# Retention plus Mish MLP: the first two tiles regrouped into the first chunks of eight batches

## The chip, the cores and the metric

The kernel runs on one core of a Trainium2 chip. The metric is device time in microseconds (us) of one execution. One profiled execution gives the trace; three others, not profiled, give the time.

The engines are named as the profile names them: PE (TensorE, matrix products; its weight loads are PEld), DVE (VectorE), ACT (ScalarE), POOL (GpSimd) and SP (SyncE, which only issues DMAs here). DMAs are issued from SP, ACT and POOL and are carried out by 16 DMA engines.

## The reference

Inputs are q, k and v of shape (8 batches, 8 heads, 576 positions, 64) in float32, and two weights, 512 x 2048 and 2048 x 512.

```python
scores = (q @ k.transpose(0, 1, 3, 2)) / sqrt(64)
gamma  = 1 - 2.0 ** (-5 - arange(8))                  # one decay per head
Dmat   = where(i >= j, gamma[h] ** (i - j), 0)
x      = ((scores * Dmat) @ v)                        # retention, no softmax
x      = x.transpose(0, 2, 1, 3).reshape(4608, 512)   # tokens x (heads * 64)
h      = x @ w_in                                     # 4608 x 2048
out    = (h * tanh(log1p(exp(h)))) @ w_out            # Mish, then 4608 x 512
```

## The kernel before

**Chunks and tiles.** Each batch has four chunks of 128 positions (c = 0 to 3) and a rest of 64; the rests of two neighbouring batches make one chunk (c = 4). That is 36 chunks, in the order b0: 0, 1, 2, 3; b1: 0, 1, 2, 3; the rests of b0 and b1; b2: 0 and so on (lines 50 to 55). Four chunks in this order make a tile of 512 tokens, the moving size of the first GEMM; there are 9 tiles.

**Attention of one chunk** is done in chunked form: the scores inside the chunk with a causal mask, plus the product of q with a state, the sum of k and v outer products of the earlier chunks of the batch. The decay is put into q and v: q is multiplied by gamma^position (and the scale), v by gamma^-position. The steps have letters in `att` (line 300):

- P, `step_p` (line 155): VectorE multiplies q by its decay into bf16 (`qks`, first half).
- V, `step_v` (161): GpSimd multiplies v by its decay into `vs`; for the first four chunks it also casts k.
- T, `step_t` (170): q and k are transposed into `qkT`. For chunks below `NPE = 16` PE does it through PSUM and ACT copies the result (line 180); for the others a DMA transpose on ACT's queue does it (line 182).
- S, `step_s` (185): PE makes the scores of all heads, two heads at a time on the two halves of its rows; VectorE multiplies them by the mask into `sm` (line 197).
- K, `step_k` (202): PE adds the chunk's outer products to the state in PSUM, ACT copies the state twice into `ssb`, with the unwanted half of each head pair set to zero (line 219).
- O, `step_o` (222): PE adds state times q (unless c = 0) and `vs` times `sm`; VectorE copies the result into `xT`, the transposed input of the first GEMM (line 243).

**The two GEMMs.** `g1(t, f)` (line 249) makes one block of 128 of the 2048 hidden columns for tile t, in 4 matmuls of 512 columns; ACT applies Mish while it moves the block into `gT`. `g2(t, i)` (line 258) makes a quarter of the sum for one chunk of 128 tokens, in 4 matmuls; after the fourth quarter the result is copied to `res` and stored by SP (`store`, line 287). G1 below stands for all 16 `g1` of a tile, G2 for all 16 `g2`.

**Loads.** `load(n)` (line 82) fetches q, k and v of a chunk, in rows of 256 bytes (64 float32 of one head and position). The first four chunks are loaded by SP, 12 DMAs in a row; every later one by GpSimd, whose DMA also casts k to bf16. The weights are loaded by GpSimd with a cast, in four parts each (lines 107 to 111). Buffers for 8 chunks of q and v and for 12 of `qks` let loads run `PF = 7` chunks ahead.

**Order.** The schedule is written out by hand (`manual_schedule`): each engine runs its instructions in the order of the program text.

1. Lines 307 to 317: attention of tile 0, chunk by chunk, between it the parts of w_in.
2. Lines 318 to 323: loads of chunks 4 to 6 and parts of w_out are issued, and G1 of tile 0 runs alone.
3. Lines 325 to 346: three of the four output chunks of tile 0 are accumulated side by side (matmuls at line 343), and attention of chunks 4 to 7 is done between them.
4. Lines 348 to 370: the last output chunk of tile 0, G1 of tile 1 and attention of chunks 8 to 11.
5. Lines 381 to 417: for t = 2 to 9, `g1(t, i)` and `g2(t - 1, i)` alternate, and the attention of the next tile, two chunks per half loop, is placed between them. For t = 2 a table of steps (line 387) brings the loop into this rhythm.
6. Line 418: the last output chunk, in two halves.

Of the kernel before, what the change touches and what calls it, by code (L numbers as in the profile page):

```python
# [10 lines left out]
F32 = mybir.dt.float32  # L11
# [6 lines left out]
def kernel(  # L18
# [28 lines left out]
    NPE = 16  # L47


    chunks = []  # L50
    for b2 in range(0, B, 2):
        for b in (b2, b2 + 1):
            for c in range(4):
                chunks.append((b, c))
        chunks.append((b2, 4))
    nT = len(chunks) // NCH
# [3 lines left out]
    io = ctx.enter_context(tc.tile_pool(name="io", bufs=8))  # L60
# [13 lines left out]


# [5 lines left out]

    def load(n):
        if n >= len(chunks):
            return
        b, c = chunks[n]
        qr = io.tile([P, H, D], F32, name="qraw")
        vr = io.tile([P, H, D], F32, name="vraw")
        qks = io.tile([P, 2, H, D], BF16, name="qks", bufs=12)
        live[n] = {"q": qr, "v": vr, "qks": qks}
        if n < NCH:  # L90
            kr = io.tile([P, H, D], F32, name="kraw", bufs=NCH)
            for t, src in ((qr, q), (kr, k), (vr, v)):
                nc.sync.dma_start(  # L93
                    out=t, in_=src[b, :, ds(P * c, P), :].rearrange("h p d -> p h d"))
            live[n]["k"] = kr
            return
        for t, src in ((qr, q), (qks[:, 1], k), (vr, v)):
            if c < 4:
                nc.gpsimd.dma_start(  # L99
                    out=t, in_=src[b, :, ds(P * c, P), :].rearrange("h p d -> p h d"))  # L100
            else:
                for e in range(2):
                    nc.gpsimd.dma_start(
                        out=t[ds(64 * e, 64)],
                        in_=src[b + e, :, ds(512, 64), :].rearrange("h p d -> p h d"))
# [7 lines left out]
    PF = 7  # L113
    for n in range(NCH):
        load(n)


    ident = consts.tile([P, P], BF16)
# [6 lines left out]
                   allow_small_or_imprecise_dtypes=True)  # L125
    ex = consts.tile([P, 5, H], F32)
    for h in range(H):
        nc.vector.tensor_scalar(ex[:, :, h], pos, math.log(1.0 - 2.0 ** (-5.0 - h)), None, op0=OP.mult)
# [8 lines left out]
    mask = consts.tile([P, P], F32)  # L137
    mask2 = consts.tile([P, P], F32)
    nc.gpsimd.memset(mask, 1.0)
    nc.gpsimd.affine_select(out=mask, in_=mask, compare_op=OP.is_ge, fill=0.0,  # L140
                            base=0, pattern=[[1, P]], channel_multiplier=-1)
    nc.gpsimd.tensor_copy(mask2, mask)
    nc.gpsimd.memset(mask2[0:64, 64:P], 0.0)

# [3 lines left out]
    nc.vector.memset(diag[64:P, 1:2], 1.0)  # L148


    st_ps = {}
    st_sb = {}
    xts = {}

    def step_p(n):
        qr = live[n]["q"]
        c = chunks[n][1]
        nc.vector.tensor_tensor(live[n]["qks"][:, 0], qr,  # L158
                                gq[:, c, :].unsqueeze(2).to_broadcast([P, H, D]), op=OP.mult)

    def step_v(n):
        vr = live[n]["v"]
        if n < NCH:
            nc.gpsimd.tensor_copy(live[n]["qks"][:, 1], live[n]["k"])
        c = chunks[n][1]
        vs = tok.tile([P, H, D], BF16, name="vs")
        nc.gpsimd.tensor_tensor(vs, vr, gv[:, c, :].unsqueeze(2).to_broadcast([P, H, D]), op=OP.mult)  # L167
        live[n]["vs"] = vs

    def step_t(n):  # L170
        flat = live[n]["qks"].rearrange("p i h d -> p (i h d)")
        qk = tr.tile([P, 2, NP, P], BF16, name="qkT", bufs=5)
        if n < NPE:
            if n < NCH:
                tp = ps_h.tile([P, 2 * NP, P], BF16, name="hp")
            else:
                tp = ps_sc.tile([P, 4 * NP, P], BF16, name="sc")[:, 0:2 * NP]
# [3 lines left out]
        else:  # L181
            nc.scalar.dma_start_transpose(out=qk.rearrange("p i n t -> p (i n) t"), in_=flat)  # L182
        live[n]["qk"] = qk

    def step_s(n):

# [8 lines left out]
        sm = tr.tile([P, 2, NP, P], BF16, name="sm")  # L195
# [6 lines left out]
    def step_k(n):  # L202

        if n >= len(chunks):
            return
        b, c = chunks[n]
        if c == 4:
            return
        ks, vs = live[n]["qks"][:, 1], live[n]["vs"]
        if c == 0:  # L210
            st_ps[b] = ps_st.tile([P, NP, 64], F32, name="st")
        st = st_ps[b]
# [4 lines left out]
        ssb = tr.tile([P, NP, 2, 64], BF16, name="ssb", bufs=8)  # L217
        for e in range(2):
            nc.scalar.activation(ssb[:, :, e, :], st, AX.Copy, scale=diag[:, e:e + 1])  # L219
        st_sb[b, c] = ssb  # L220

    def step_o(n):

        b, c = chunks[n]
        t, s = divmod(n, NCH)
        qk, vs, sc, sm = (live[n][x] for x in ("qk", "vs", "sc", "sm"))
        del live[n]
        ot = sc[:, 0]
        if c > 0:
            halves = [(0, P, b, c - 1)] if c < 4 else [(0, 64, b, 3), (64, 64, b + 1, 3)]  # L230
            for i0, iw, bb, cc in halves:
                for p in range(NP):
                    for e in range(2):
                        nc.tensor.matmul(ot[ds(64 * e, 64), p, ds(i0, iw)], lhsT=st_sb[bb, cc][:, p, e, :],  # L234
                                         rhs=qk[:, 0, p, ds(i0, iw)],
                                         start=(i0 == 0 and p == 0), stop=False, skip_group_check=True)
# [212 lines left out]
```

## Time and profile before

| What | Value |
|---|---|
| Median of three runs | 325.55 us (325.14 to 325.85) |
| Span of the profiled execution, first to last instruction | 323.8 us |
| PE busy | 302.4 us, 93% |
| GpSimd busy | 139.2 us, 43% |
| ACT busy | 131.3 us, 41% |
| VectorE busy | 113.0 us, 35% |
| DMA | 43.36 MB, mean 134 GB/s |
| HBM read, written | 36.70 MB, 9.44 MB |
| Start of G1 of tile 0 | 22.34 us |
| Start of the loop for t = 2 | 84.73 us |

The profiled execution has no other time of its own than the span; the three runs lie 1.3 to 2.0 us above it, for what lies before the first and after the last instruction. A busy PE is not a PE at its peak, as matmuls overlap: the spacing of neighbouring matmuls tells their price, 0.216 us for 512 columns where nothing is in the way. The bytes that the profile counts for a DMA with a cast are those written.

The parts of the profile used below: the slices (busy tenths of an engine in 40 equal parts of the span), windows (busy time by engine, then granted clock, DMA share and GB/s), the timeline (instructions with start and length), and the chain of waits (what released the work that ended last, step by step back to the start).

### The profile page before, as it was taken

The page shows a single profiled execution, that of the slowest core. Times are in us where ns is not written, and L with a number is a line of the kernel's source. Part 1 is how long each engine was busy: PE and PEld are TensorE (multiplying, and loading weights), DVE is VectorE, ACT ScalarE, POOL GpSimd, SP SyncE. Part 2 cuts the span into 40 slices and gives each one's busy share as a digit, 9 for nine tenths or more (in the row PEclk, how much of TensorE's full clock was granted, in tenths as well). Part 3 has the DMA queues.
Part 4 walks back from the last instruction along what each step waited for, and adds up shares of the span by engine and source line. Part 5 has one row for each costly group of instructions (what it writes and reads, how often), then busy time and mean ns, then how long its engine had stood idle before and what let it go on. Part 6 is the DMA issues. An engine that isn't in the chain of part 4 may idle for free.

```text
span 323.8 us, 5627 instructions
## 1 busy us (share of the span) xinstructions
PE 302.4 (93%) x2345; PEld 150.3 (46%) x2384; DVE 113.0 (35%) x154; ACT 131.3 (41%) x232; POOL 139.2 (43%) x168
## 2 busy tenths in 40 slices
PE   1779999989999899999999999999999999999995
PEld 1544445444545445444544454445444444444444
DVE  2640055354544425152425343443434232000111
ACT  5435734367746324334434432334243432333200
POOL 4596858999998717372717184202010000000000
PEclk9999999999999999999999999999999999999999
DMA  9999999999999979979999999404040401000031
GB/s 171 215 165 215 227 213 196 254 226 181 172 217 212 189 145 119 174 131 191 111 173 106 203 90 197 105 32 99 32 99 32 100 32 34 32 32 34 33 97 65
DMA packets 81833, 43.36 MB, mean 134 GB/s; under 512 B 68880, under 2 KB 73232, under 8 KB 81808
## 3 DMA queue, kind: packets, MB, share of 16 engines
q0 software_dynamic: 42816, 25.17, 51.8%
q1 hardware_dynamic: 17728, 12.46, 14.5%
q10 hardware_dynamic: 21264, 5.38, 12.3%
q8 instruction: 18, 0.29, 0.4%
q14 instruction: 7, 0.06, 0.1%
HBM read 36.70 MB, written 9.44 MB: 142 GB/s over the span
## 4 chain that ended last, share of the span: by engine, by line
PE 85%; DVE 6%; issue 2%; SPq 2%; DMA 2%; ACT 2%; ACTq 1%; POOL 0%; DVEq 0%
PE hp L254 37%; PE ops L269 31%; DVE sm L197 3%; PE sc L193 3%; PE sc L239 2%; PE sc L234 2%; PE hp L269 2%; SPq L93 2%; PE sc L179 2%; PE st L215 2%; DVE qks L158 2%; DMA kraw<-in_k_dram 2%; PE hp L343 1%; PE hp L281 1%; ACTq L182 1%
## 5 line engine op out<-in xcount | busy, mean ns | idle before, releaser
L254 PE MATMUL hp<-xT,w_in_t 128*128 128x512 bf16 x544 | 143.7, 384 | 3.9 <-DVE xT L243 1.0
L256 ACT ACTIVATE gT<-hp 128x512 bf16<-128x512 f32 x144 | 84.9, 597 | 134.3 <-PE hp L254 100.8
L269 PE MATMUL ops<-w_out_t,gT 128*128 128x512 bf16 x477 | 122.2, 379 | 1.2 <-ACT res L289 0.7
L254 PEld LDWEIGHTS <-w_in_t 128*128 128x128 bf16 x576 | 54.1, 99 | 65.3 <-issue 5.2
L269 PEld LDWEIGHTS <-gT 128*128 128x128 bf16 x512 | 50.0, 98 | 61.6 <-issue 2.0
L289 DVE COPY res<-ops 128x512 f32<-128x512 f32 x30 | 20.7, 691 | 144.8 <-PE ops L269 140.7
L167 POOL TENSOR_TENSOR vs<-vraw,gv 128x512 bf16<-128x512 f32 x36 | 38.7, 1080 | 40.4 <-PE sc L239 24.0
L197 DVE TENSOR_TENSOR sm<-sc,mask 128x1024 bf16<-128x1024 f32 x36 | 42.8, 1217 | 18.7 <-PE sc L193 18.7
L99 POOL DMA_DIRECT2D qraw<-in_q_dram x28 | 26.2, 934 | 36.4 <-DVE qks L158 35.6
L219 ACT ACTIVATE ssb<-st,diag 128x256 bf16<-128x256 f32 x64 | 26.8, 470 | 23.4 <-PE st L215 23.4
L243 DVE CAST xT<-sc 128x512 bf16<-128x512 f32 x36 | 23.7, 686 | 22.0 <-PE sc L239 21.9
L158 DVE TENSOR_TENSOR qks<-qraw,gq 128x512 bf16<-128x512 f32 x36 | 25.4, 731 | 11.6 <-DMA qraw<-in_q_dram 11.6
L99 POOL DMA_DIRECT2D vraw<-in_v_dram x28 | 25.6, 914 | 1.2 <-DMA w_in_t<-in_moe_w_in_dram 0.8
L99 POOL DMA_DIRECT2D qks<-in_k_dram x28 | 25.5, 911 | 0.9 <-DMA w_out_t<-in_moe_w_out_dram 0.9
L180 ACT COPY qkT<-sc 128x1024 bf16<-128x1024 bf16 x12 | 12.1, 1012 | 11.7 <-PE sc L179 11.7
L179 PEld LDWEIGHTS <-qks 128*128 128x128 bf16 x128 | 8.5, 106 | 13.6 <-DVE qks L158 10.0
L193 PE MATMUL sc<-qkT 64*128 64x128 bf16 x288 | 13.1, 227 | 1.9 <-ACT qkT L180 1.6
L239 PE MATMUL sc<-sm,vs 128*64 128x128 bf16 x288 | 14.6, 230 | 0.0
L193 PEld LDWEIGHTS <-qkT 64*128 64x128 bf16 x288 | 8.6, 98 | 11.3 <-issue 7.6
L234 PE MATMUL sc<-qkT,ssb 128*64 128x128 bf16 (+1 forms) x256 | 12.0, 224 | 1.1 <-DVE sm L197 1.0
L215 PE MATMUL st<-vs,qks 128*64 128x64 bf16 x256 | 10.5, 206 | 0.7 <-ACT ssb L219 0.4
L239 PEld LDWEIGHTS <-vs 128*64 128x64 bf16 x288 | 10.6, 117 | 1.0 <-issue 1.0
(44 smaller groups left out, 101.0 us busy)
## 6 DMA issues: line engine op xcount, KB each, us to landing
out_dram<-res SPq DMA_DIRECT2D x31, 256.0 KB, 2.0
qraw<-in_q_dram POOLq DMA_DIRECT2D x28, 256.0 KB, 6.0
vraw<-in_v_dram POOLq DMA_DIRECT2D x28, 256.0 KB, 6.4
qks<-in_k_dram POOLq DMA_DIRECT2D x28, 128.0 KB, 6.2
w_in_t<-in_moe_w_in_dram POOLq DMA_DIRECT2D x4, 512.0 KB, 6.5
w_out_t<-in_moe_w_out_dram POOLq DMA_DIRECT2D x4, 512.0 KB, 11.3
qraw<-in_q_dram SPq DMA_DIRECT2D x4, 256.0 KB, 5.0
kraw<-in_k_dram SPq DMA_DIRECT2D x4, 256.0 KB, 5.1
```

Of the source, the lines that this page charges most:

```text
L99: nc.gpsimd.dma_start(out=t, in_=src[b, :, ds(P * c, P), :].rearrange("h p d -> p h d"))
L158: nc.vector.tensor_tensor(live[n]["qks"][:, 0], qr, gq[:, c, :].unsqueeze(2).to_broadcast([P, H, D]), op=OP.mult)
L167: nc.gpsimd.tensor_tensor(vs, vr, gv[:, c, :].unsqueeze(2).to_broadcast([P, H, D]), op=OP.mult)
L193: nc.tensor.matmul(sc[:, e, p, :], lhsT=qk[r, 1, p, :], rhs=qk[r, 0, p, :], start=True, stop=True)
L197: nc.vector.tensor_tensor(sm.rearrange("p e n i -> p (e n) i"), sc.rearrange("p e n i -> p (e n) i"), m.unsqueeze(1).to_broadcast([P, 2 * ...
L219: nc.scalar.activation(ssb[:, :, e, :], st, AX.Copy, scale=diag[:, e:e + 1])
L239: nc.tensor.matmul(ot[ds(64 * e, 64), p, :], lhsT=vs[:, 2 * p + e, :], rhs=sm[:, e, p, :], start=(c == 0 and p == 0), stop=True, skip_grou ...
L243: nc.vector.tensor_copy(xts[t][:, :, ts(s, P)], ot)
L254: nc.tensor.matmul(hp, lhsT=w_in_t[:, c, ts(f, P)], rhs=xts[t][:, c, :], start=(c == 0), stop=(c == KC - 1))
L256: nc.scalar.activation(gts[t][:, f, :], hp, AX.Mish)
L269: nc.tensor.matmul(ops, lhsT=gts[t][:, f, ts(s, P)], rhs=w_out_t[:, f, :], start=(f == 0), stop=(f == nF - 1))
L289: copy(ot, ops)
```

## The change

**Chunks.** The first chunks (c = 0) of all eight batches now come first: chunks 0 to 7, which are tiles 0 and 1. After them follow c = 1, 2, 3 of each batch and the rests. A first chunk has no state before it.

**First chunks.** Tiles 0 and 1 no longer go through `att`. For four batches at once, q and k are loaded by head, with partitions that hold four neighbouring positions of one batch, so that each row has 1 KB. They land in the memory of a `gT` buffer (`stage`). The decay is no longer put into q and v but into a mask per head (`dmask`), which is multiplied into the scores; v is only cast. v is loaded after q and k. All of these loads are issued by SP. The steps work by pair of heads p: cast, transposes (which also put the positions back in order), scores; and then by batch: output. For the state, v is multiplied by its decay as before (`f_state`), and k in bf16 is put back into chunk form by DMAs inside SBUF, on SP (`f_k`).

**Filler.** `keep_warm` issues matmuls on zeros, 28 in all, between the first steps of tile 0.

**Loads.** For the later chunks q and v are issued by SP, k by GpSimd. `PF` is 5 instead of 7, with fewer buffers. From chunk 12 on (`NPE = 12`) the transposes are DMA transposes, on SP instead of ACT.

**Order.** Attention of tile 0; loads of tile 1 behind a VectorE memset that follows tile 0's output; G1 of tile 0 with attention of tile 1 in it (at f = 6 to 14); G1 of tile 1; G2 of tile 0 with attention of chunks 8 to 11; then the loop as before, with the state steps placed by `state(upto)`, which makes the next state in a fixed order if it is needed by then. Tile 0's results are copied by ACT.

```diff
-    NPE = 16
-    chunks = []
+    NPE = 12
+    PF = 5
+    chunks = [(b, 0) for b in range(B)]
     for b2 in range(0, B, 2):
         for b in (b2, b2 + 1):
-            for c in range(4):
+            for c in range(1, 4):
                 chunks.append((b, c))
         chunks.append((b2, 4))
...
+    stage = gp.tile([P, 2, H, 4 * D], F32, name="gT")
+    qf, kf = stage[:, 0], stage[:, 1]
+    def load_first(t):
+        for p in range(NP):
+            for dst, src in ((qf, q), (kf, k)):
+                for h in (2 * p, 2 * p + 1):
+                    nc.sync.dma_start(
+                        out=dst[:, h, :],
+                        in_=src[ds(4 * t, 4), h, 0:P, :].rearrange("b (g r) d -> g b (r d)", r=4))
+        for b in range(4 * t, 4 * t + 4):
+            v0[b] = io.tile([P, H, D], F32, name="vraw")
+            nc.sync.dma_start(out=v0[b], in_=v[b, :, 0:P, :].rearrange("h p d -> p h d"))
...
+    for h in range(H):
+        nc.scalar.activation(dmask[:, h, :], dist, AX.Exp, scale=lg[h], bias=lnd[:, 0:1])
...
+    def keep_warm(n):
+        for _ in range(n):
+            nc.tensor.matmul(idle, lhsT=zeros[:, 0:P], rhs=zeros, start=True, stop=True)
...
+    def f_transpose(t, p, copies):
...
+            for r in range(4):
+                nc.tensor.transpose(tps[i][:, r, :],
+                                    fst[t][name][:, r, ds(2 * p, 2), :].rearrange("p h d -> p (h d)"), ident)
+            copies[i](out_t.rearrange("p b (g r) -> p b g r", r=4),
+                      tps[i].rearrange("p r (g b) -> p b g r", b=4))
+    def f_scores(t, p):
...
+        nc.vector.tensor_tensor(sm, sc, dmask[:, ds(2 * p, 2), :].unsqueeze(2).to_broadcast([P, 2, 4, P]),
+                                op=OP.mult)
+    def f_out(t, b, copy):
...
+        copy(xts[t][:, :, ts(b, P)], ot)
+    def f_k(t, b):
...
+        for r in range(4):
+            nc.sync.dma_start(out=k0[n][ds(r, 32, step=4)].rearrange("p h d -> p (h d)"),
+                              in_=fst[t]["kb"][ds(b, 32, step=4), r].rearrange("p h d -> p (h d)"))
...
-        for t, src in ((qr, q), (qks[:, 1], k), (vr, v)):
+        for t, src, queue in ((qks[:, 1], k, nc.gpsimd), (qr, q, nc.sync), (vr, v, nc.sync)):
...
-            nc.scalar.dma_start_transpose(out=qk.rearrange("p i n t -> p (i n) t"), in_=flat)
+            nc.sync.dma_start_transpose(out=qk.rearrange("p i n t -> p (i n) t"), in_=flat)
...
+    f_cast(0, 0, 0, dve)
+    f_cast(0, 0, 1, pool)
+    for p in range(1, NP):
+        f_cast(0, p, 0, pool)
+        f_cast(0, p, 1, pool)
+        if p == 2:
+            make_masks()
+    load_w_in(0)
+    keep_warm(8)
+    for p in range(NP + 1):
+        if p < NP:
+            f_transpose(0, p, (act, act))
+            keep_warm(3)
+        if p > 0:
+            f_scores(0, p - 1)
+            keep_warm(2)
+    f_v(0, 0, pool)
+    f_v(0, 1, act)
+    load_w_in(1)
+    f_v(0, 2, pool)
+    f_v(0, 3, dve)
+    for b in range(4):
+        f_out(0, b, (dve, act)[b % 2])
...
+    load_w_in(2)
     load_w_in(3)
+    nc.vector.memset(stage[0:1, 0, 0, 0:1], 0.0)
+    load_first(1)
+    for b in range(4):
+        f_state(0, b)
+        f_k(0, b)
+    for i in range(4):
+        load_w_out(i)
+    for p in range(NP):
+        f_cast(1, p, 0, pool)
+        f_cast(1, p, 1, pool)
+    for b in range(4):
+        f_v(1, b, pool)
+    for b in range(4):
+        f_state(1, b)
+        f_k(1, b)
+    for f in range(nF):
+        if f in (6, 8, 10, 12):
+            f_transpose(1, (f - 6) // 2, (dve, dve))
+        if f in (8, 10, 12, 14):
+            f_scores(1, (f - 8) // 2)
+        g1(0, f)
+    for b in range(4):
+        f_out(1, b, dve)
+    for n in range(N0, N0 + PF):
+        load(n)
+    for f in range(nF):
+        g1(1, f)
+        if f == 8:
+            state(N0)
+    att(N0, "PV")
     for i in range(nF):
-        g1(0, i)
...
+        n, w = N0 + i // 4, i % 4
         if w == 0:
             att(n, "T")
         elif w == 1:
             if i > 4:
                 att(n - 1, "O")
         elif w == 2:
-            att(n, "SK")
+            att(n, "S")
+            state(n + 1)
         else:
             att(n + 1, "PV")
-            load(n + 4)
-        g1(1, i)
+            load(n + PF)
+            state(n + 1)
+        g2(0, i)
     att(3 * NCH - 1, "O")
-    queued = [3 * NCH + 4]
+    queued = [3 * NCH + PF - 1]
```

In the loop for t = 2 to 9 the steps P, V, T, S and O and the loads stay at their places; the K steps become calls of `state`.

## The prediction

> **What bounds the kernel now.** I read the page first (busy shares, slices), then windows of 1 us over the head, its timeline, the chain of waits from 60 to 155 us, and the rows of the loads and of the DMA transposes.
>
> ```profile
> span 323.8 us, 5627 instructions
> PE 302.4 (93%) x2345; PEld 150.3 (46%) x2384; DVE 113.0 (35%) x154; ACT 131.3 (41%) x232; POOL 139.2 (43%) x168
> PE   1779999989999899999999999999999999999995
> DMA  9999999999999979979999999404040401000031
> ```
> TensorE is the bound from about 110 us on. What can be won lies in the first third, and there the DMA digits are nine as well.
>
> ```profile
> 14.00:15.00 1.00, 0.89 (x18) 0.65 (x16) 0.11 (x1) 0.90 (x1) 1.00 (x2) 1.00 1.35 217
> 24.00:25.00 1.00, 1.00 (x4) 0.45 (x3) 0.00 (x0) 0.60 (x1) 1.00 (x2) 1.00 1.22 204
> ```
> The last column is GB/s, in bytes written. At 14 us only loads with rows of 256 B run: 217 GB/s, so 256 KB (one of q, k, v of a chunk) take 1.2 us of all 16 DMA engines. At 24 us weights run: 204 GB/s of bf16, so one of the eight weight loads (512 KB written, 1 MB read) takes 2.6 us.
>
> ```profile
> 12.28 1.14 SPq L93 DMA_DIRECT2D vraw<-in_v_dram  x1
> 14.78 0.95 POOL L108 DMA_DIRECT2D w_in_t<-in_moe_w_in_dram  x1
> 22.34 0.59 PE L254 MATMUL hp<-xT,w_in_t 128*128 128x512 bf16 x1 [0.78 <-DVE xT L243]
> 26.99 4.91 PEld L254 LDWEIGHTS <-w_in_t 128*128 128x128 bf16 x23 [0.27 <-issue]
> ```
> The first GEMM of tile 0 (G1) starts at 22.34. From 26.99 its weight loads stand 4.91/23 = 0.214 us apart; in the timeline before that, they stand 0.427 apart. Some 11 matmuls cost double: 2.3 us.
>
> ```profile
> 65.19 1.07 POOL L167 TENSOR_TENSOR vs<-vraw,gv 128x512 bf16<-128x512 f32 x1
> 66.18 0.94 POOL L99 DMA_DIRECT2D qraw<-in_q_dram  x1
> 67.11 0.90 POOL L99 DMA_DIRECT2D qks<-in_k_dram  x1
> 67.98 0.90 POOL L99 DMA_DIRECT2D vraw<-in_v_dram  x1
> ```
> GpSimd spends 2.7 us of each chunk's 3.7 on issuing loads, without a gap. In the chain beside it VectorE's q scaling takes 1.31 us instead of 0.68:
>
> ```profile
> 76.58 1.31 DVE qks L158
> ...
> 84.73 1.04 PE hp L254 x4
> ...
> 106.80 2.44 ACTq L182
> ...
> 119.97 0.55 PE sc L193 x16
> ...
> 151.63 0.55 PE sc L193 x16
> ```
> At 84.73 the loop for tile 2 begins, at 119.97 that for tile 3, at 151.63 that for tile 4: 35.2 us, then 31.6 without waits. 84.73 is my mark: by then both kernels have done the same (G1 of tiles 0 and 1, the second GEMM, G2, of tile 0, attention of 12 chunks).
>
> ```profile
> L182 ACTq DMA_TRANSPOSE qkT<-qks x20: 1246/1248/2438, 106.8 to 252.3; - x20
> DMA to landing us min/median/max: 3.1/5.3/9.0
> ```
>
> **The change part by part.**
>
> *First tile.* Sixteen q, k loads of 128 KB on SP. The nearest issues are the stores, also of 128 rows, 0.33 us each: 6 us in all. The rate of 1 KB rows is not in the trace. Per engine a 256 B row takes 18.8 ns at 217 GB/s and a 2 KB read 80 ns; in a straight line 1 KB takes 45 ns, so 2 MB take 5.8 us (bounds 5.2 at the rate of the 2 KB rows, 9.6 at that of 256 B). First bytes move at 2.0, q and k are through at 7.9, the four v at 12.7 if undisturbed. The casts on GpSimd (0.61 each, the masks' 1.0 among them) end at 10.3; only then w_in's first part is issued, 4.5 us earlier than at 14.78. Transposes 0.61, ScalarE copies of 0.55, scores 0.35 and the mask product 1.22 put the last masked scores at 13.1. The last v cast stands ahead of VectorE's copies of xT, so G1 starts at 17.1 if v lands at 13.7, and at 22 if v waits for two weight loads. I take 19.1, one weight load beside it. The 28 filler matmuls (0.43 or 0.22 each, 6 to 12 us) lie in TensorE's waits for rows; without that cover they hold the scores of each pair of heads back by up to 2.1 us.
>
> The row on the clock is the 0.427 against 0.214. The Trainium skill, page "TensorE: Matmul & The Clock Gate", Part 1, says that the clock doubles after a busy window of about 3.4 us and falls back after an idle one. By it the filler warms the array, but the wait for v3 (13.6 to 18) can cool it again, and the 2.3 us would stay; by the row alone I would let them go. Neither enters the sum, for the next reason.
>
> *The start of G1 does not carry through.* G1 of tile 1 now follows G1 of tile 0, and needs all of tile 1. Its 3 MB go out on SP only after the memset behind xT on VectorE, at 19.1 (nothing of tile 1 is behind that memset on VectorE yet), while GpSimd's queue holds the rest of the weights. Whatever the shares, v of tile 1 is last in SP's queue, so DMA work adds up: 2.0 + 5.8 + 4.8 (tile 0) + 4x2.6 (w_in) + 4x2.3 (w_out: the first lands 2.3 after the v ahead of it) + 5.8 + 4.8 = 42.8, landing 0.9 later at 43.7. As a test, the same sum for before, 2.0 + 12x1.2 + 4x2.6 + 2x2.3 and three chunks at 3.15 (q 1.2, k 0.8, v 1.15 between landings), gives 40.9 + 0.9 for v of chunk 6; it landed at 42.9. Then v cast 0.61, output 0.25, copy 0.69, hand-overs 0.25: G1 of tile 1 starts at 45.5. Bounds: 42, if SP gets half the time and part of w_out comes after; 49, if casts, transposes and scores follow the rows serially. TensorE's own work to there (13.8 + 8 chunks at 1.15) fits. GpSimd has four v scalings (1.07) and four w_out issues (0.8) ahead of tile 1's casts, done at 22.5, before the first rows land. The 16 regrouping DMAs of k stand behind v on SP; the state that reads them comes in the middle of G1 of tile 1. Chunks 8 to 12 load under that G1, 5x3.15 = 15.8 us; the first is needed at 60.
>
> *G1 of tile 1, then G2 of tile 0 with attention.* 64 matmuls at 0.216 = 13.8, a state and the start 0.5: 59.8. Then 13.8, four chunks at 1.5 (transposes 0.45, scores 0.35, output 0.45, state 0.25), the wait for xT 0.95, and 0.1 to 0.6 per chunk where mask product and q scaling (1.22 + 0.68) outlast the matmuls beside them (1.98): 21.9. GpSimd has two issues less per chunk, so the q scaling counts 0.68 here. Tile 2's loop starts at 81.7 instead of 84.73: **-3.0**.
>
> The row that sizes both first tiles is 217 GB/s at 256 B. The page "DMA: Bandwidth & Descriptors", Specifications, has rows from 512 B at line rate and a ceiling of 435 GB/s; by an estimate from that page 2 MB take 4.8 us, and the sum would be 2 us lower. No run here shows 1 KB rows yet.
>
> *DMA transposes from chunk 12, on SP.* Gone: 32 transposes on TensorE, 4x0.45 = 1.8 us of tile 2's loop, and ScalarE's hold of 2.44 at 106.8, the cause of most of the other 1.8 that this loop loses (35.2 - 31.6 = 3.6). New: SP serves loads, stores and transposes in order. The transpose of chunk 12 stands behind the last store of tile 0 (copy 0.58, issue 0.33): 1.3 after G2 ends. That of chunk 13 stands behind q and v of chunks 16 (which the counters load a second time) and 17, 4x0.44 at SP's price with an empty queue (1.14 when full). So it is issued at 1.3 + 1.25 + 1.76 = 4.3 and lands 5.3 later, at 9.6; scores of 13 are due at 6.8 (output 0.45, xT 0.95, three rounds of 1.73, a state). Wait: 2.8. That of chunk 15 stands behind the load of chunk 19, whose buffer the q scaling of chunk 15 frees, 3.4 after scores 13 (mask product, a copy, the scaling); then four issues, a store, a transpose: it lands 12.0 after scores 13 and is due at 10.4. Wait: 1.6. Bounds: landing in 3.1 with cheap issues leaves 1.4 + 0.5; full-queue issues and the loads' 4.6 us ahead of each pair make 7 + 4.3. I take 4.4, by the median landing. Tile 2's loop: 31.6 + 4.4 = 36.0, **+0.8**. In later halves of a loop (15.8 us) a transpose lands some 11.5 after the scores before it: hidden by 4 us, which is also what it would take to cost again.
>
> *The rest.* The decay masks (8 exponentials of about 0.24 on ScalarE) are hidden by the wait for the first rows. ScalarE's stores of tile 0 (0.58) fill the place that Mish has left in that phase. Loads run 5 chunks ahead instead of 7, 39 us at 7.9 a chunk, against a landing of 6. Tiles 3 to 8 and the end stay.
>
> **Sum.** -3.0 + 0.8 = -2.2: a span of 321.6. Around the profiled span of 323.8 lie 1.3 to 2.0 us (three runs, 325.14 to 325.85), so against their median of 325.55 I predict 323.3.
>
> **Rivals.**
> 1. *Slower: SP's order.* Place: the transposes of chunks 13 and 15. Price: waits of 7 + 4.3 = 11.3 instead of 4.4, 330.2. For it: SP's issues at 1.14 in a full queue; on ScalarE's queue no loads stood ahead. Against: landings of 3.1. It decides once the two waits pass 6.6 us.
> 2. *Tile 1's rows come later*, the weights first and then all serially: G1 of tile 1 at 49, 326.8. For it: weights alone saturate the DMA. Against: v is last in any order, and casts can run as rows land.
> 3. *More gain*: G1 of tile 1 at 42.5, 3.0 sooner, and transposes that land in 3.1 (1.9 of waits, 2.5 less): 317.8. For it: 1 KB rows may run at the weights' rate. Against: the loads ahead of the transposes.
>
> **How the numbers follow.** A measurement here can tell about 0.2%, 0.65 us. Forecast 0.38 (its own range 321 to 326.2; 0.27 faster, 0.06 same, 0.05 slower); rival 1 0.25, all slower; rival 2 0.17 (0.03, 0.03, 0.11); rival 3 0.20, all faster. That is faster 0.50, same 0.09, slower 0.41. The range, 317 to 331.5, reaches from rival 3 to just past rival 1.
>
> **What would show it.** First G1 matmul near 19; TensorE waiting for tile 1's casts inside G1 of tile 0; G1 of tile 1 near 45.5, released by VectorE's last copy; tile 2's loop near 81.7; waits for qkT near 88 and 98, of 2.8 and 1.6. It is wrong if GpSimd's casts set the pace rather than the rows, if 1 KB rows run no faster than 256 B ones, or if SP's queue stalls in later tiles too.

## The result, and the profile after

The changed kernel takes 350.78 us, the median of five runs (350.52 to 353.91), against 325.14 us (324.62 to 325.85) for the kernel before: a ratio of 1.0805, with a 95% interval of 1.0766 to 1.0845. The forecast was 323.3 us with a range up to 331.5, so the change is slower by 25.6 us where a gain of about 2 us was expected. The profiled execution is the one of 353.91 us, the slowest of the five (the other four took 350.5 to 351.2); its span is 352.2 us, 28.4 more than before.

The page of the changed kernel, first lines and slices:

```profile
span 352.2 us, 5825 instructions
PE 311.0 (88%) x2342; PEld 152.0 (43%) x2380; DVE 110.0 (31%) x156; ACT 130.5 (37%) x241; POOL 86.7 (25%) x112
...
PE   5927678979970999999999999999999999999995
...
PEclk9987898999996799999999999999999999999999
DMA  4999974989999999995979788991723220020022
```

PE has about as many matmuls as before and is busier by only 8.6 us, but its share falls from 93% to 88%. The digits say where (a slice is 8.8 us): slice 3 shows 2, slices 4 to 9 (26 to 79 us) mostly 6 to 8, slices 12 and 13 (97 to 114 us) 7 and 0. The clock digits fall to 6 and 7 just there and after. From slice 14 on TensorE is full. The DMA digits start with a 4, where the kernel before had nines: in the first 9 us the loads in rows of 1 KB do not keep the DMA engines busy.

SP's timeline, with the start, the length, the line and the number of issues:

```profile
0.81 1.34 SPq L101 DMA_DIRECT2D gT<-in_q_dram  x2
...
11.25 3.43 SPq L106 DMA_DIRECT2D vraw<-in_v_dram  x4
26.43 1.19 SPq L101 DMA_DIRECT2D gT<-in_q_dram  x2
...
47.95 22.96 SPq L231 DMA_DIRECT2D k<-kb  x32
71.01 1.57 SPq L248 DMA_DIRECT2D qraw<-in_q_dram  x1
...
101.19 2.90 SPq L276 DMA_TRANSPOSE qkT<-qks  x1
...
109.55 2.34 SPq L276 DMA_TRANSPOSE qkT<-qks  x1
```

The first 16 loads take from 0.81 to 11.2 us, 0.65 us each. Line 231 is the one to look at: the 32 DMAs that put k of the first chunks back into chunk form hold SP's queue for 23 us, and the first load of a later chunk, q of chunk 8, is issued behind them at 71.0. The transposes of chunks 12 and 13 come 8.4 us apart, with the loads of chunks 16 and 17 between them.

TensorE's timeline; in the brackets stands the idle time before the instruction and what ended it:

```profile
26.75 0.59 PE L355 MATMUL hp<-xT,w_in_t 128*128 128x512 bf16 x1 [0.67 <-ACT xT L219]
...
57.52 0.53 PE L355 MATMUL hp<-xT,w_in_t 128*128 128x512 bf16 x1 [0.79 <-DVE qraw L245]
...
76.19 0.62 PE L273 MATMUL sc<-ident,qks 128*128 128x128 bf16 x8 [2.64 <-DVE qks L258]
...
98.55 1.02 PE L355 MATMUL hp<-xT,w_in_t 128*128 128x512 bf16 x4 [0.79 <-DVE xT L345]
...
109.01 0.61 PE L286 MATMUL sc<-qkT 64*128 64x128 bf16 x8 [5.12 <-DMA qkT<-qks]
114.36 0.61 PE L286 MATMUL sc<-qkT 64*128 64x128 bf16 x8 [4.74 <-DMA qkT<-qks]
```

G1 of tile 0 starts at 26.75 (22.34 before), G1 of tile 1 at 57.5, chunk 8 at 76.2 after a wait, the loop for tile 2 at 98.55 (84.73 before). Then come the two waits for transposes, 9.9 us together.

The chain of waits joins the two pictures. From 13.66 on it runs through the last v load of tile 0, from 29.6 through two loads of tile 1's rows (9.62 and 7.21 us to land), from 47.95 through all 32 issues of line 231, and then:

```profile
13.66 10.25 DMA vraw<-in_v_dram
...
70.32 0.59 SPq L231
71.01 4.33 DMA qraw<-in_q_dram
75.44 0.70 DVE qks L258
...
101.19 7.78 DMA qkT<-qks
...
109.55 4.76 DMA qkT<-qks
```

TensorE was the engine to watch in the kernel before. Here, over the first 125 us, the chain stands more than a quarter of its time on SP's issuing and about a third on DMAs in flight.

### The profile page after: what moved, and what is told of

The parts are those of the page before. It is cut to its first block, busy times and chain, and to the rows that moved or that the text cites. A ratio compares the mean times of both kernels' runs of the same rounds, so it can differ in the third digit from the quotient of the medians.

```text
span 352.2 us, 5825 instructions
## 1 busy us (share of the span) xinstructions
PE 311.0 (88%) x2342; PEld 152.0 (43%) x2380; DVE 110.0 (31%) x156; ACT 130.5 (37%) x241; POOL 86.7 (25%) x112
## 2 busy tenths in 40 slices
DMA packets 140123, 46.65 MB, mean 132 GB/s; under 512 B 126144, under 2 KB 135616, under 8 KB 140096
## 4 chain that ended last, share of the span: by engine, by line
PE 66%; DMA 17%; SPq 11%; issue 2%; ACT 2%; DVE 1%; POOL 0%; ACTq 0%; DVEq 0%; POOLq 0%
PE ops L370 28%; PE hp L355 25%; DMA qkT<-qks 8%; SPq L231 6%; DMA gT<-in_q_dram 5%; PE hp L370 4%; SPq L101 4%; DMA vraw<-in_v_dram 3%; PE sc L286 2%; PE st L318 2%; ACT ssb L322 1%; PE sc L336 1%; DMA qraw<-in_q_dram 1%; PE sc L341 1%; PE hp L381 1%
## 5 line engine op out<-in xcount | busy, mean ns | idle before, releaser
L370 PE MATMUL ops<-w_out_t,gT 128*128 128x512 bf16 x492 | 126.8, 381 | 0.4 <-PE st L318 0.2
L264 POOL TENSOR_TENSOR vs<-vraw,gv 128x512 bf16<-128x512 f32 x28 | 29.3, 1048 | 148.0 <-issue 89.7
L290 DVE TENSOR_TENSOR sm<-sc,mask 128x1024 bf16<-128x1024 f32 x28 | 33.1, 1216 | 18.7 <-PE sc L286 18.7
L258 DVE TENSOR_TENSOR qks<-qraw,gq 128x512 bf16<-128x512 f32 x28 | 18.2, 682 | 18.0 <-DMA qraw<-in_q_dram 18.0
L345 DVE CAST xT<-sc 128x512 bf16<-128x512 f32 x28 | 18.2, 686 | 10.7 <-PE sc L341 10.6
L370 PE MATMUL hp<-w_out_t,gT 128*128 128x512 bf16 x61 | 14.7, 379 | 0.4 <-issue 0.3
L160 PE MATMUL ops<-zeros 128*128 128x512 bf16 x27 | 11.0, 529 | 1.3 <-DVE zeros L111 1.3
L199 DVE TENSOR_TENSOR sm<-sc,dmask 128x1024 bf16<-128x1024 f32 x8 | 9.7, 1218 | 7.7 <-PE sc L197 7.7
L336 PE MATMUL sc<-qkT,ssb 128*64 128x128 bf16 (+1 forms) x256 | 11.2, 215 | 0.0
L336 PEld LDWEIGHTS <-ssb 128*64 128x64 bf16 x256 | 7.8, 111 | 2.5 <-issue 2.5
L225 POOL TENSOR_TENSOR v0s<-vraw,gv 128x512 bf16<-128x512 f32 x8 | 8.4, 1072 | 1.5 <-DMA vraw<-in_v_dram 1.5
```

The costliest lines, as they stand in the source:

```text
L258: nc.vector.tensor_tensor(live[n]["qks"][:, 0], live[n]["q"], gq[:, c, :].unsqueeze(2).to_broadcast([P, H, D]), op=OP.mult)
L264: nc.gpsimd.tensor_tensor(vs, live[n]["v"], gv[:, c, :].unsqueeze(2).to_broadcast([P, H, D]), op=OP.mult)
L290: nc.vector.tensor_tensor(sm.rearrange("p e n i -> p (e n) i"), sc.rearrange("p e n i -> p (e n) i"), m.unsqueeze(1).to_broadcast([P, 2 * ...
L370: nc.tensor.matmul(ops, lhsT=gts[t][:, f, ts(s, P)], rhs=w_out_t[:, f, :], start=(f == 0), stop=(f == nF - 1))
```

## The experiments

Twelve kernels were run. A ratio is always against the kernel before, measured beside the kernel in question (324.4 to 325.1 us). Where no base is named, the edit was made to the changed kernel. "Scores 8" is the time at which the scores of chunk 8 start: 78.5 in the changed kernel, 64.05 in the kernel before. It is read from one trace of each kernel. Where the program is the same up to that point (the three kernels of section 2), it lies between 78.35 and 79.64.

### 1. Is it the 32 DMAs that hold chunk 8?

Four of them stay; the other 28 are issued behind the loads of chunks 8 to 12.

```diff
         f_state(0, b)
-        f_k(0, b)
+        if b == 0:
+            f_k(0, b)
...
         f_state(1, b)
-        f_k(1, b)
...
         load(n)
+    for b in range(1, 2 * NCH):
+        f_k(b // NCH, b % NCH)
```

> Only 28 of the 32 regrouping DMAs of k (all but those of batch 0) are moved behind the loads of chunks 8 to 12. Theory SP-issue (the 32 DMAs hold SP for 23 us, 48 to 71, and chunk 8's q stands behind them): chunk 8's q is issued at 57.5, where its memset frees it, instead of 71.0; the transposes of chunk 8 start at 71.8, the end of G1 of tile 1, instead of 76.2; total 4 to 8 us less, 343 to 347. Rival (the DMA engines or GpSimd's k loads set chunk 8's time anyway): T of chunk 8 stays at 75 to 76, total 350 to 351.

Measured: 359.19 us, ratio 1.1065 (1.1037 to 1.1093). q of chunk 8 is issued at 56.8 instead of 71.0 and scores 8 stand at 73.3, 5.2 us earlier: the queue was what held chunk 8. But the 28 DMAs cost the same wherever they stand. SP's timeline, then TensorE's:

```profile
72.76 20.08 SPq L231 DMA_DIRECT2D k<-kb  x28
```

```profile
98.88 1.86 PE L355 MATMUL hp<-xT,w_in_t 128*128 128x512 bf16 x4 [3.11 <-ACT res L389]
115.97 0.61 PE L286 MATMUL sc<-qkT 64*128 64x128 bf16 x8 [11.80 <-DMA qkT<-qks]
```

Now the stores of tile 0 and the transpose of chunk 12 stand behind them: the wait for that transpose is 11.8 us instead of 5.1, and the kernel loses 8.4 us where a gain was expected. The theory was right on chunk 8 and had the same blind spot one step later.

The same DMAs can be taken away altogether. Here k of the first chunks is read a second time from HBM, by eight casting loads on GpSimd:

```diff
-        for r in range(4):
-            nc.sync.dma_start(out=k0[n][ds(r, 32, step=4)].rearrange("p h d -> p (h d)"),
-                              in_=fst[t]["kb"][ds(b, 32, step=4), r].rearrange("p h d -> p (h d)"))
+        nc.gpsimd.dma_start(out=k0[n], in_=k[n, :, 0:P, :].rearrange("h p d -> p h d"))
```

The calls move as well: those of tile 0 behind tile 1's casts, those of tile 1 behind the loads of chunks 8 to 12.

> The changed kernel with only the regrouping of k replaced by 8 casting loads on GpSimd; DMA transposes from chunk 12 stay. Theory backlog (the transposes of chunks 12 and 13 landed late because the loads had started 13 us late behind the regrouping): the waits before the scores of 12 and 13 fall from 9.8 to 4 or less, total 338 to 341. Rival (transposes are late by their place in the loop): the waits stay at 9 to 10, total 344 to 347.

Measured: 348.06 us, ratio 1.0723 (1.0675 to 1.077). Scores 8 stand at 72.3 and the loop for tile 2 starts at 92.4, 6.2 us earlier in the trace; the medians differ by 2.7. The two traces exaggerate the difference, as this one is of the fastest of its four executions (346.26 to 349.58) and that of the changed kernel of the slowest of five. The waits for the transposes stay as they were, 5.30 and 4.74 us, as the rival said. So these waits do not come from the 32 DMAs.

### 2. What makes the transposes late?

SP's order was my first rival. If it were the cause, the transposes would come in time from a queue with no loads in it:

```diff
-            nc.sync.dma_start_transpose(out=qk.rearrange("p i n t -> p (i n) t"), in_=flat)
+            nc.scalar.dma_start_transpose(out=qk.rearrange("p i n t -> p (i n) t"), in_=flat)
```

> The DMA transposes go back to ScalarE's queue, nothing else. Theory SP-order (they stand behind loads and a store on SP): the waits of 5.1 and 4.7 us before the scores of chunks 12 and 13 shrink to 2 together, the clock does not drop, total 340 to 343. Rival (the DMA engines are full, share 1.56 from 100 to 110): the transposes still take 7 to 8 us to land, total 348 to 351.

Measured: 353.88 us, ratio 1.088 (1.0827 to 1.0933). ACT issues them at 99.8 and 102.1, 2.3 us apart; the scores that need them:

```profile
107.72 0.40 PE L286 MATMUL sc<-qkT 64*128 64x128 bf16 x8 [1.40 <-DMA qkT<-qks]
112.67 0.61 PE L286 MATMUL sc<-qkT 64*128 64x128 bf16 x8 [4.55 <-DMA qkT<-qks]
```

Issued 7.4 us earlier than on SP, the second transpose lands only about 1.7 us earlier: it takes 10.5 us from issue to landing, and the first 7.9, while loads for the chunks ahead are in flight. Later scores in this tile wait another 1.08 and 1.66 us. The order of SP's queue shifts the wait; it does not make it. What makes it is that a DMA transpose is used at all in this stretch. That the loads in flight are what makes it slow is likely (over all 20 transposes of the kernel before, the median to landing is 5.3 us), but no run took the loads away.

The opposite edit puts the transposes of chunks 12 to 15 on TensorE, as in the kernel before:

```diff
-    NPE = 12
+    NPE = 16
```

> Chunks 12 to 15 are transposed by TensorE again. Theory SP-order at the entry of the loop (the first DMA transposes are needed 5 us after the last store): TensorE gets 1.8 us more work and loses 9.8 us of waits and the half clock after them, total 340 to 343. Rival (the waits only move on to chunks 16 and 17, the new first ones): total 347 to 351.

Measured: 343.72 us, ratio 1.0585 (1.0557 to 1.0613), 7.1 us faster than the changed kernel. All waits for transposes in that tile are gone; scores 12 and 13 run as one group at 105.3. So it is the DMA transposes of these four chunks that cost.

The counter that loads chunk 16 a second time was tried by itself:

```diff
-    queued = [3 * NCH + PF - 1]
+    queued = [3 * NCH + PF]
```

> The changed kernel without the second load of chunk 16 (the counter starts at 17). Theory (the transpose of chunk 13 stands behind four load issues on SP, two of them needless): it is issued 2 to 3 us sooner and the load of chunk 19 no longer waits for chunk 15, total 347 to 349. Rival (the DMA engines' backlog decides, 3.1 us of it are this load): the same or more, 346 to 348; if neither matters, 350 to 351.

Measured: 351.38 us, ratio 1.083 (1.08 to 1.086): no gain. One of the two waits goes (0.40 left at scores 12), the other grows to 5.60. This run says more about something else, as G1 of tile 0 happened to start at 22.28 in it:

```profile
53.40 7.97 PE L355 MATMUL hp<-xT,w_in_t 128*128 128x512 bf16 x36 [0.79 <-DVE qraw L245]
...
74.35 1.04 PE L273 MATMUL sc<-ident,qks 128*128 128x128 bf16 x8 [6.58 <-DVE qks L258]
```

A start 4.5 us earlier gives a G1 of tile 1 that is 4.1 us earlier, and then TensorE waits 6.58 us instead of 2.64 for chunk 8. Scores 8 stand at 78.65, where they stood. SP's timeline of this run shows why:

```profile
36.75 10.37 SPq L106 DMA_DIRECT2D vraw<-in_v_dram  x4
47.17 22.80 SPq L231 DMA_DIRECT2D k<-kb  x32
```

Tile 1's rows are issued from 21.96 on, 4.5 us sooner, but the four v behind them now take 10.37 us to issue instead of 5.29, with the DMA engines at a share of 1.2. The 32 DMAs start at 47.17, nearly where they stood (47.95), and chunk 8 follows them.

### 3. The two together, and the order of the tiles

On the kernel with `NPE = 16`, k was read from HBM in the way shown above.

> On top of the run with TensorE transposes up to chunk 15: k of the first chunks is read a second time from HBM, in chunk form, by 8 casting loads on GpSimd, instead of 32 regrouping DMAs on SP. Theory SP-order (in the run that moved these 32 DMAs they cost 20 us of SP wherever they stand): chunk 8's scores move from 78.4 to 74 or earlier, no later stall takes their place, total 4 to 8 us below that run's 343.7, 336 to 340. Rival (DMA engines full from 72 on, the loads themselves): total 342 to 345.

Measured: 338.46 us, ratio 1.0435 (1.0388 to 1.0482), 5.3 us better than with `NPE = 16` alone; scores 8 at 71.9 (78.35 there), the loop for tile 2 at 91.97 (99.60 there). With the transposes on TensorE, the loss by the 32 DMAs shows more clearly: 5.3 us, as the theory had it. The edit also adds eight loads, so this is the worth of the exchange.

On that kernel, G2 of tile 0 was put ahead of G1 of tile 1, with tile 1's attention beside G2, and chunks 8 and 9 loaded ahead of the rest:

```diff
     for f in range(nF):
-        if f in (6, 8, 10, 12):
-            f_transpose(1, (f - 6) // 2, (dve, dve))
-        if f in (8, 10, 12, 14):
-            f_scores(1, (f - 8) // 2)
         g1(0, f)
+    for i in range(nF):
+        if i in (1, 4, 8, 11):
+            f_transpose(1, (1, 4, 8, 11).index(i), (dve, dve))
+        if i in (3, 6, 10, 13):
+            f_scores(1, (3, 6, 10, 13).index(i))
+        g2(0, i)
...
-    for f in range(nF):
-        g1(1, f)
-        if f == 8:
-            state(N0)
+    state(N0)
     att(N0, "PV")
...
-        g2(0, i)
+        g1(1, i)
```

> On top of the run with TensorE transposes to chunk 15 and k from HBM: the order of the kernel before comes back. G2 of tile 0 runs first, with attention of tile 1 in it, then G1 of tile 1 with attention of chunks 8 to 11; the loads of chunks 8 and 9 are issued without their memset. Theory order (G1 of tile 1 cannot start before tile 1's rows, 55.4 there, and TensorE has only G1 of tile 0 until then): G1 of tile 1 still starts near 55, but G2 of tile 0 lies before it, the loop for tile 2 starts near 80 instead of 92, total 325 to 329 instead of 338.5. Rival (the weights for G2 come too late, and G2 only waits where G1 waited): total 334 to 338.

Measured: 337.42 us, ratio 1.0381 (1.0316 to 1.0447). The loop for tile 2 starts at 89.9 instead of 92.0, where 80 was expected. The intervals of the two kernels overlap, so the order of the tiles is worth little: G1 of tile 0 now runs without a gap (64 matmuls in 15.0 us from 27.2 on), but four waits of 0.8 us for copies move into G2.

The loads of q and v from chunk 10 on were then put back on GpSimd:

```diff
-        for t, src, queue in ((qks[:, 1], k, nc.gpsimd), (qr, q, nc.sync), (vr, v, nc.sync)):
+        qv = nc.sync if n < N0 + 2 else nc.gpsimd
+        for t, src, queue in ((qks[:, 1], k, nc.gpsimd), (qr, q, qv), (vr, v, qv)):
```

> As the run with G2 first, but q and v from chunk 10 on are issued by GpSimd, as before the change. Theory of the run that moved only these loads to SP (4.7 us slower, since its loads took DMA time from the weights): here the weights are in before chunk 10 loads, so no difference, within 2 us of that run. Rival (SP's queue of loads, stores and transposes costs in later tiles too): 3 to 5 us less than that run.

Measured: 341.47 us, ratio 1.0497 (1.0447 to 1.0548), 4 us worse, which neither theory had. GpSimd scales v too late: TensorE waits 4.41 us for `vs` until 75.9. That GpSimd's casts and added issues delay it is argued from the program. In this order of the work, SP is the better place for these loads.

### 4. One part of the change alone, in the kernel before

In the kernel before, only q and v of the later chunks were moved to SP:

```diff
-        for t, src in ((qr, q), (qks[:, 1], k), (vr, v)):
+        for t, src, queue in ((qr, q, nc.sync), (qks[:, 1], k, nc.gpsimd), (vr, v, nc.sync)):
             if c < 4:
-                nc.gpsimd.dma_start(
+                queue.dma_start(
```

> The kernel before with one part of the change alone: q and v of all later chunks are issued by SP, k by GpSimd. Theory that this part gains by itself (GpSimd was busy without a gap from 61 to 103 and slowed the q scaling): 321 to 324. Rival (stores and loads in one SP queue, or the DMA engines were the limit anyway): 324.5 to 328.

Measured: 329.18 us, ratio 1.0139 (1.0093 to 1.0184): slower by 4.8 us, by itself. The issues on the page, with the median us to landing as the last column, in this kernel and in the kernel before:

```profile
w_out_t<-in_moe_w_out_dram POOLq DMA_DIRECT2D x4, 512.0 KB, 22.0
```

```profile
w_out_t<-in_moe_w_out_dram POOLq DMA_DIRECT2D x4, 512.0 KB, 11.3
```

The weights land twice as late, and TensorE waits for w_out in G2 of tile 0 (1.52 us until 45.3, and three waits of 0.5 to 0.8). Two causes are possible, and no run separates them. On one queue the weights and the chunks went in the order in which GpSimd issued them; on two queues they are in flight side by side. But the queue also changes the packets. The page of this kernel, then that of the kernel before:

```profile
DMA packets 143273, 43.36 MB, mean 133 GB/s; under 512 B 134416, under 2 KB 138768, under 8 KB 143248
```

```profile
DMA packets 81833, 43.36 MB, mean 134 GB/s; under 512 B 68880, under 2 KB 73232, under 8 KB 81808
```

The same bytes go in 1.75 times as many packets: GpSimd's queue loses 5248 packets with these loads and SP's gains 66688. From 20 to 45 us, with the DMA engines full in both kernels, they move 192 GB/s instead of 214. The changed kernel has 140123 packets. The packets alone do not decide: putting q and v back on GpSimd in the swapped order lowered them from 142683 to 90842, and that kernel became slower. The price of an issue on GpSimd, 2.7 us a chunk, looked like a cost in the profile before; this run shows that taking it away gains nothing by itself.

### 5. The start

First, the filler was left out (its results are used by nothing):

```diff
     def keep_warm(n):
-        for _ in range(n):
+        for _ in range(0):
```

> The 28 filler matmuls on zeros are left out of the changed kernel. Theory of the prediction (they lie in waits and do not carry through, since v3 comes at 23.9): total 349 to 352, G1 of tile 0 at 26 to 27 and at half rate as before. Rival (they hold the scores back, or they do keep the clock): scores of the first pair at 10 instead of 11.8 and total 347 to 349; or, if their warmth counts, 353 to 356.

Measured: 350.89 us, ratio 1.0817 (1.0776 to 1.0859): no difference. G1 of tile 0 starts at 22.0 here, nearly 5 us sooner, and nothing of it is left at the end: the 32 DMAs start at 47.89 and scores 8 stand at 77.7. Whether the sooner start is owed to the filler is not shown, as in kernels that keep it G1 starts anywhere from 22.3 to 27.4.

Then the weights were issued only after all four casts of v, so that no weight load runs beside v (and the last cast goes from VectorE to GpSimd):

```diff
-    load_w_in(0)
     keep_warm(8)
...
     f_v(0, 1, act)
-    load_w_in(1)
     f_v(0, 2, pool)
-    f_v(0, 3, dve)
+    f_v(0, 3, pool)
+    load_w_in(0)
+    load_w_in(1)
```

> The first two weight loads are issued by GpSimd only after all four v of tile 0 are cast. Theory packets (weight packets of 2 KB alternate with v's of 256 B, so v3 took 10.2 us to land): v3 lands 4 to 5 us after its issue, by 16 to 18; G1 of tile 0 starts near 21 instead of 26.75, then waits for weights; the loads of tile 1 start 5 us sooner; total 345 to 348. Rival (v3 is slow by its own 256 B rows, or the weights are needed as early as they come): G1 starts at 26 or later, total 351 to 356.

Measured: 355.36 us, ratio 1.094 (1.0908 to 1.0972). The last v is no longer what G1 waits for; w_in is (4.01 us), and G1 starts at 24.87. All weights are then later, the 32 DMAs start at 52.05, 4.1 us later than in the changed kernel, and scores 8 stand at 81.8, 3.3 us later. With v first, the weights are late; with the weights beside it, v is late.

Last, ACT issued the k rows of tile 0, so that two queues share the 16 issues:

```diff
-            for dst, src in ((qf, q), (kf, k)):
+            for dst, src, queue in ((qf, q, nc.sync), (kf, k, nc.sync if t else nc.scalar)):
                 for h in (2 * p, 2 * p + 1):
-                    nc.sync.dma_start(
+                    queue.dma_start(
```

> Only the issuing queue of tile 0's k rows changes: ScalarE's instead of SP's, so two queues issue 8 DMAs each. Theory issue price (0.64 us per issue on SP bounds the first 12 us, 197 to 209 GB/s): the last q, k rows land by 9 instead of 13.3, v is issued 5 us earlier and is through before the first weight packets, v3 lands by 15 instead of 23.9, G1 of tile 0 starts at 19 to 20; total 344 to 348. Rival (1 KB rows move no faster than 209 GB/s): rows land at 12 to 13 as before, G1 at 25 or later, total 349 to 352.

Measured: 350.40 us, ratio 1.0787 (1.0745 to 1.083), the same as the changed kernel. The v loads are issued at 8.0 to 12.4 instead of 11.25 to 14.7. One row of the windows from here settles what the changed kernel left open:

```profile
4.00:6.00 2.00, 0.68 (x3) 0.00 (x0) 0.00 (x0) 0.00 (x0) 0.06 (x1) 1.00 0.97 299
```

Only rows of 1 KB are in flight here, and they move 299 GB/s (275 in the next 2 us), against 197 and 207 in the same windows of the changed kernel. So issuing had set the pace there; the rival had the total right but not its reason. Each issue takes longer, 0.89 us on SP, but two queues work side by side. The gain is lost again soon: ACT's eight issues push back its exponentials for the decay masks (9.06 instead of 3.89), the first scores come at 17.2 instead of 11.8, and G1 starts at 26.7. It is not a clean test of the start.

## Why the prediction was wrong

The account, against the profiled spans of 321.6 (predicted) and 352.2 us:

| Stretch | Predicted | Measured | Difference |
|---|---|---|---|
| To G1 of tile 1 | 45.5 | 57.5 | +12.0 |
| From there to the transposes of chunk 8 | 14.3 | 18.7 | +4.4 |
| From there to the loop for tile 2 | 21.9 | 22.4 | +0.5 |
| Loop for tile 2 | 36.0 | 45.0 | +9.0 |
| From scores of chunk 16 to the last scores | 142.9 (as before) | 147.6 | +4.7 |
| The end | 61.0 (as before) | 61.0 | 0 |

**First tile: the price of an issue was taken from the wrong row.** I priced the 16 loads by the stores, 0.33 us each. They cost 0.65, so that issuing, not moving, sets the pace: in the first windows the DMA engines run at a share of 0.57 and 0.72, at 161 and 209 GB/s, and with two queues the same loads reached 299. Windows of the changed kernel (clock, DMA share and GB/s last):

```profile
2.00:4.00 2.00, 2.00 (x6) 0.76 (x5) 0.51 (x8) 1.39 (x2) 0.34 (x2) 1.00 0.57 161
8.00:10.00 2.00, 2.00 (x13) 1.17 (x11) 0.00 (x0) 1.14 (x3) 1.17 (x2) 1.00 0.72 209
...
44.00:46.00 2.00, 1.08 (x8) 0.50 (x6) 1.32 (x2) 1.19 (x2) 0.84 (x2) 1.00 1.20 303
```

q and k were through near 13.3 instead of 7.9. My estimate for these rows, 2 MB in 5.8 us or 362 GB/s, lies above what was seen of them over 2 us. The Trainium skill's page "DMA: Bandwidth & Descriptors", Specifications, gives line rate from rows of 512 B on; the 299 GB/s with two queues lie above the 217 of the 256 B rows, and no run here shows a line rate. The last v is issued at 13.66, just ahead of the first weights at 13.90, and takes 10.25 us to land; I had counted one weight load beside it, and its upper bound of 22 was too low by 5. The wait for v3, 5.32 us long, cooled the clock as the Trainium skill's page "TensorE: Matmul & The Clock Gate", Part 1, has it: the granted clock is 0.50 from 24 us and the weight loads of G1 stand 0.43 us apart until about 30. The late start of G1 was of no consequence by itself: where G1 happened to start near 22 (the filler left out, the counter mended), scores 8 stood within 0.9 us of the same place, and the total was the same.

**"The start of G1 does not carry through" was right, and the sum of DMA work behind it was too small.** I let that sum hold tile 1 (43.7 us). The last v of tile 1 landed at 53.1. Its rows were issued from 26.43 on, 7.3 us later than I had them, but that is not the reason: in the two runs where they were issued at 21.7 and 22.0, the last v was ready at 52.3 and 51.5, and the DMA engines ran at a share of about 1.2 from 16 to 48 us. With 13.3 in place of 7.9 for the first rows my sum gives 49.1. By this sum 5.4 us of the 9.4 are the price of an issue again; the rest stays open.

**The 32 DMAs.** Not even this alone sets the time of chunk 8. The step that failed is "The 16 regrouping DMAs of k stand behind v on SP", costed at nothing. There are 32, not 16 (four for each of eight chunks), and I looked at who waits for their data, the state in G1 of tile 1, and not at what is queued behind them: all loads from chunk 8 on. They take 0.64 to 0.72 us each and hold SP for 23 us. I had put the loads of chunks 8 to 12 "under that G1"; they could not start before it was nearly over. The two runs of the first experiment and the combination in the third show it: without them chunk 8 comes 5 to 6.5 us sooner. And in the seven traces with all 32 in place (the changed kernel and six others), scores 8 follow the first of them by 29 to 31.5 us, whether it is issued at 46.05 or at 52.05. In the total the exchange for eight loads was worth 5.3 us with the transposes on TensorE, and 2.7 with them on the DMA.

**G1 of tile 1 and G2 with attention** were nearly right: 16.0 us without the wait for chunk 8 (predicted 14.3; at a granted clock of 0.82 in its first part) and 22.4 (predicted 21.9).

**Transposes.** The waits came at chunks 12 and 13, where I had 13 and 15, and they were larger: 9.9 us instead of 4.4, close to the 11.3 of my first rival. That is partly luck, as the rival named the wrong cause: from ACT's queue, without SP's order, the waits of this tile came to 8.7. I took the landing time of 5.3 us from a median over transposes that run mostly late in the kernel, where loads are rare. Between 100 and 115 us it was 7.8 and 4.8 from SP, and 7.9 and 10.5 from ACT, where no loads stand ahead in the queue. TensorE pays a second time, as the clock falls after such a wait: it is 0.55 on average from 110 to 120 us. Moving these transposes to the DMA, which I had counted as 1.8 us of TensorE's time saved, cost 7.1 us in all, as the run with `NPE = 16` shows. In the later tiles the transposes are hidden, as I had it.

**The mark at 84.73 was no mark.** I wrote that by then "both kernels have done the same". They have not: the first chunks need no state, so the states they make are made later. State matmuls (line 215 before, 318 after) behind the mark, in windows:

```profile
84.73:262.78 178.05, 6.59 (x168) 4.42 (x168) 1.00 0.79 129
```

```profile
98.55:291.22 192.67, 8.28 (x208) 5.94 (x208) 0.97 0.85 136
```

That is 40 more (five states), and the products of q with a state go from 152 to 200. At the busy times of these rows it makes 3.7 us (1.7 and 2.0), of work that lay ahead of the mark before. It accounts for most of the 4.7 us that the later tiles take longer, and a little of the loop for tile 2. That it costs this much is argued from the counts; no run changed it.

**What stays open.** The two steps that runs undid, the transposes and the 32 DMAs, are worth 12.3 of the 25.6 us (350.78 to 338.46). With the tiles swapped as well, 12.9 us are still missing against the kernel before. The move of q and v to SP cost 4.8 us in the kernel before, by the order of the queues or by the packets, and 3.7 us of state work lies behind the mark. But the one run that put these loads back, in the swapped order, became slower. In the swapped order G1 of tile 0 starts at 27.2, 4.9 us later than before, and scores 8 stand at 69.8, 5.8 later; there, with the 32 DMAs gone, the start may carry through after all. I have not separated it from the two queues.

## What to carry to other kernels

When work moves to another queue, count its DMAs and ask what stands behind them there, not only who needs their data: here 32 small DMAs of 32 KB at 0.64 to 0.72 us each, off every data path that I followed, held the load of chunk 8 for 13.6 us (from 57.4, when its buffer was free, to 71.0). A single queue that looks overloaded may be worth keeping: with these loads on a second queue the weights landed twice as late, by the lost order or by the smaller packets. And a point that "both kernels reach with the same work done" has to be counted by instruction before a difference is taken at it.

## What the runs showed of the hardware that I had not expected

- The time of an issue on SP did not follow the bytes: 0.60 us for a 128 KB load in rows of 1 KB and 0.59 for a 32 KB copy inside SBUF, with 0.04 between two, and 0.33 for a store of 256 KB to 128 rows in the kernel before. Nor is it fixed: the same 128 KB loads took 0.89 each where ACT issued beside SP, and the four v of tile 1, 256 KB each in rows of 256 B, took 10.37 us together where the DMA engines were at a share of 1.2.
- Rows of 1 KB moved 299 GB/s when two queues issued them, and 197 to 209 from SP alone. Rows of 256 B moved 217 in the kernel before. In the window 44 to 46 of the changed kernel, the last rows of 1 KB and the first of v together moved 303.
- The q and v of the later chunks went in 66688 packets from SP's queue and in 5248 from GpSimd's, for the same bytes (difference of two pages).
- The last v of tile 0, beside casting weight loads on another queue, took 10.25 us to land in the changed kernel and 5.0 in the run with the counter mended, which has the same program up to there.
- In the kernel before the page printed a granted clock of 1.00 while the weight loads of its first G1 stood 0.427 us apart; in the changed kernel the same spacing goes with a printed 0.50.
